# An early transpose of wqkv, kept in DRAM, and three more row buffers

## The chip, the cores and the metric

The kernel runs on one core of a Trainium2 chip. The metric is device time in microseconds (us) from launch to end of the program. The core has five engines with a queue each: TensorE (PE, matrix products; PEld is its weight load), VectorE (DVE), ScalarE (ACT), GpSimd (POOL) and SyncE (SP, which computes nothing). SP, POOL and ACT also start DMA transfers, which 16 DMA engines carry out. An instruction that waits holds everything behind it on its own queue.

## The reference

A transformer block and its gradients: sliding-window attention (32 heads of 16, a window of 8 positions two apart), then a GELU feed-forward, with 2048 positions and width 512, in bf16.

```python
qkv = (layernorm(x) @ wqkv)            # q, k, v of 32 heads
logits = q[s] . k[s - 2*w] * scale     # w = 0..7, masked where s - 2*w < 0
o = sum_w softmax(logits)[w] * v[s - 2*w]
h  = x + o @ wo
h2 = h + gelu(layernorm(h) @ w1 + b1) @ w2 + b2
# returned: h2 and, from grad_out, the gradients of x, wqkv, wo, w1, b1, w2, b2
```

The backward part is what the change touches. For each position the gradients of q, k and v are window sums: products of attention weights (or of their gradients) with rows of k, q or grad-of-o, summed over the window. Then `gx = gq @ wq^T + gk @ wk^T + gv @ wv^T`, which needs `wqkv` transposed, and the gradient of `wqkv` is `layernorm(x)^T` times these gradients.

## The kernel before

The 2048 positions are cut into four chunks of 512 (`c` = 0 to 3). A tile framework places the instructions: the program names tiles with a pool, a tag and a number of buffers, the framework adds the semaphore waits, and a scheduler orders each engine's queue. `high_priority` moves some matmuls ahead, and `gate(ins, key)` makes one instruction wait for a marked one, so that a transfer does not begin too early. Pools are stacks of memory on a left and a right side; a tile of a later pool may lie where a released one lay, and then waits for its last readers.

The order of the work:

- Forward, by chunk: layernorm, qkv, attention, output projection, feed-forward. `wqkv` stands in SBUF with its columns reordered; after the second last attention chunk it is written to `wqkv_d` in DRAM (line 580).
- Backward through the feed-forward: `b1_gg(i)` (lines 660 to 697) goes over seven pairs of hidden tiles. For each it loads `bu` and `bs` on POOL's queue (four buffers each), makes the GELU derivative on ACT and DVE (the ACT instruction of line 675 is marked `("y", i, f2)`), multiplies with a TensorE product, transposes the result on TensorE and stores it as `h1tm_d` on POOL's queue. `b1_gx(i)` is the product with `w1` transposed and the layernorm backward. Between them `gw2_gen` makes the gradient of `w2`; each of its 14 steps loads a transposed `gtm` on SP's queue (two buffers) and is 16 matmuls.
- Backward through the output projection: `b_go(c)`, with `woT`, a DMA transpose of `wo` made by `load_T` (line 725).
- Backward through the softmax: `b_ga(c)` (line 743). It loads `v4` and `go4` (named `bv` and `go` in the profile, one buffer each), makes 2 x 4 products `pag` on DVE in four buffers of tag `prA`, sums them on TensorE into `ga`, and turns them into `gl` by four DVE operations, lines 753 to 757.
- Window sums: `b_sum(c, sel)` (line 836). `sel` 2 is the value gradient (rows `go_r`), 0 the query gradient (rows `k_r`), 1 the key gradient (rows `q_r`). Each has a load of weights `ba` (two buffers; 16 small DMAs in all for `sel` 0) and four row loads `r4` (`r` in the profile, 576 KB each, `W4B` = 5 buffers of tag `w4`). Each row tile gives two DVE products of 1.2 us (`pb`, line 330) and eight matmuls (line 336).
- `b_gx(c)` (line 867) multiplies the three gradients with `wqkvT` (`psy`, line 881) and goes back through layernorm; `gwqkv_gen` and `gwo_gen` make weight gradients and, with `gw1_gen` (line 769), fill TensorE between the sums.

The loop of lines 921 to 929 does `sel` 2 for all chunks, with `b_ga(2)` after the last step of chunk 0 and `b_ga(3)` after step 1 of chunk 2; `take(wg)` places one step of `gw1_gen` per sum step. At the first step of chunk 2 it issues the load of `wqkvT` on SP: one DMA transpose of all of `wqkv_d`, 512 x 1536, gated on a copy of `gw1_gen`. After chunk 2 `load_otm` issues two loads of 1 MB on POOL. `wqkvT` lies in pool `bg`, which exists from line 828 on, when the transposed feed-forward weights are released. Pool `bp2` (line 934) lies where `bt` and `bm` lay, which hold operands of `gw1_gen` and of `b_ga`; its first loads wait for their last readers.

Of the kernel before, what the change touches and what calls it, by code (L numbers as in the profile page):

```python
# [10 lines left out]
P = 128  # L11
BF16 = mybir.dt.bfloat16
# [23 lines left out]
def kernel(  # L36
# [74 lines left out]
    def gate(ins, key):  # L111
        behind(ins, mark[key])
# [36 lines left out]
    h1tm_d = dram.tile([S, F], BF16, name="h1tm_d")  # L149
    gq_d = [[dram.tile([CH, D], BF16, name=f"gq_d{s}_{c}") for c in range(NC)] for s in range(3)]  # L150
    wqkv_d = dram.tile([D, 3 * D], BF16, name="wqkv_d")
    wo_d = dram.tile([D, D], BF16, name="wo_d")

    def tm(ap2d):
# [377 lines left out]
    def mix(gen, gen2, steps=1):  # L532
        for _ in gen:
            take(gen2, steps)
        take(gen2, 100)
# [163 lines left out]
    def b1_gx(i):  # L699
        c = b1_order[i]  # L700
        t1s = gh1.pop(c)
        for j in range(TC):
            ps = acc(f"psx{c}_{j}", "L" if i < NC - 1 else "B")
            for ft in range(FT):
                nc.tensor.matmul(ps[:], lhsT=t1s[ft // 2][:, ft % 2, j * P:(j + 1) * P], rhs=w1T[:, ft, :],  # L705
                                 start=(ft == 0), stop=(ft == FT - 1))
            t = c * TC + j
            ln_bwd(ps[:], ln2a[:, c, j, :], rstd2[:, t:t + 1], gout[c][:, j, :], gh[c][:, j, :], f"f{t}")
            yield
# [13 lines left out]
    ln2a = bm.tile([P, NC, TC, D], BF16, name="ln2a")  # L723

    def load_T(t_, d_t, key):
        gate(sync.dma_start_transpose(out=t_[:], in_=d_t[:, :]), key)

    def b_go(c):
        ghT = get(bm, [P, DC, CH], BF16, f"ghT{c}", "ghT", 1)
# [13 lines left out]
    def b_ga(c):  # L743
        v4 = feat4(bm, v_r, PAD + CJ * c - HALO, CJ + HALO, f"bv4_{c}", "k4", 1, ga_key.get(c))
        go4 = feat4(bm, go_r, CJ * c, CJ, f"go4_{c}", "q4", 1, ga_key.get(c))
        gl = get(bm, [P, Q4, TC, 2 * H], BF16, f"gl{c}", "gl", 1)
        for i in range(TC // 2):
            ga = ltile(f"ga{c}_{i}")
            dots(bm, ga, go4, v4, i, f"g{c}_{i}")
            g4 = ga[:].rearrange("p j (w h) -> p j w h", w=W)  # L750
            a4 = attn_v(c, i)
            pr = bm.tile([P, 2, W, H], F32, name=f"sp{c}_{i}", tag="e", bufs=2)
            nc.vector.tensor_tensor(out=pr[:], in0=g4, in1=a4, op=ALU.mult)
            rs = const.tile([P, 2, H], F32, name=f"rs{c}_{i}", tag="rs", bufs=2)
            nc.vector.tensor_reduce(out=rs[:], in_=pr[:].rearrange("p j w h -> p j h w"), axis=AX.X, op=ALU.add)
            nc.vector.tensor_tensor(out=pr[:], in0=g4, in1=rs[:].unsqueeze(2).to_broadcast([P, 2, W, H]), op=ALU.subtract)
            nc.vector.tensor_tensor(out=pair_v(gl, i), in0=a4, in1=pr[:], op=ALU.mult)
        put_q(pq, gl_r, c, gl[:].rearrange("p s j m -> p s (j m)"))
# [33 lines left out]

    load_ln2a(0)
    mix(b1_gx(0), none)
    for i in range(1, NC):
        load_ln2a(i)
        for n, _ in enumerate(b1_gg(i)):
            take(gw2, 1 if n in (2, 5) else 0)
            if n == 3 and i == 1:
                load_T(woT, wo_d, ("y", 1, 3))  # L800
        if i == NC - 1:
            br2.release()
            bt = pool("bt", 1)
            load_tmx(0, 2)
            load_tmx(2, 4)
            mix(b_go(0), none)
            b_ga(0)
        for n, _ in enumerate(b1_gx(i)):
            take(gw2, 1 if n == 1 else 0)
        if i > 1:  # L810
            mix(b_go(3 if i == 2 else 1), none)
# [24 lines left out]
    def b_sum(c, sel):  # L836
        sg = 0 if sel == 0 else 1
        d_a = at_r if sel == 2 else gl_r
        d_r, t_r = ((k_r, PAD - 2), (q_r, 0), (go_r, 0))[sel]
        nja = CJ + 2 * sg  # L840
        a4 = att4(bs_, d_a, CJ * c, nja, f"ba{sel}_{c}", "ba", 2, sg)
        gt = gvt[c] if sel == 2 else bp.tile([P, TC, D], BF16, name=f"gt{sel}_{c}")
        gts[sel, c] = gt
        for qd in range(Q4):
            r4 = row4(bs_, d_r, qd, t_r + CJ * c, CJ + 2, f"r4_{sel}{c}{qd}", "w4", W4B, sg)
            ps = acc(f"pss{sel}{c}_{qd}", "A")
            wsum(bs_, ps, a4, r4, sg, f"{sel}{c}_{qd}", 200)
            o_ap, i_ap = gt[:, :, qd * P:(qd + 1) * P], ps[:].rearrange("p (j m) -> p j m", j=TC)
            if sel == 2:
                mark["s", c, 2] = mark["s", c, 2, qd] = nc.scalar.copy(out=o_ap, in_=i_ap)  # L850
            else:
                mark["s", c, sel] = nc.scalar.activation(out=o_ap, in_=i_ap, func=ACT.Copy, scale=scale)  # L852
            yield
# [67 lines left out]
    for c in range(NC):  # L921
        for n, _ in enumerate(b_sum(c, 2)):
            take(wg)
            if c == 2 and n == 0:
                load_T(wqkvT, wqkv_d, ("ow1", 2, 2))
            if (c, n) in ((0, 3), (2, 1)):
                b_ga(2 + c // 2)
        if c == 2:
            load_otm()
    mix(wg, none)  # L930
    bt.release()
    bm.release()
# [66 lines left out]
```

## Time and profile before

| | |
|---|---|
| Time, median of 7 runs | 734.33 us |
| Lowest and highest | 730.05 and 736.39 us |
| The profiled execution: time / span of its instructions | 735.18 / 732.9 us |
| PE busy | 622.3 us (85%), 3551 matmuls |
| DVE busy | 554.9 us (76%) |
| ACT / POOL busy | 388.1 / 208.3 us |
| Mean granted TensorE clock | 0.959 of full speed |
| DMA | 163.57 MB, mean 223 GB/s |

Times in a profile are from the start of the span. "Busy" leaves out DMA issues, semaphores and register work. In a timeline each line gives start, duration, engine, source line, operation and "output<-inputs", with the number of instructions merged into it; a bracket gives the idle time of the engine before it and what ended it. `SPq` is SP's queue: its durations are the time the queue spent on issuing, not the transfer's. "To landing" is the time from a DMA's issue to its end. The DMA share is the mean busy share of the 16 DMA engines; it can exceed 1, since packets overlap.

The row products stand from 512 to 691 us; the feed-forward backward from about 290 to 460.

### The profile page before, as it was taken

How to read it: one execution, taken by the hardware profiler on the slowest of the kernel's cores; microseconds unless marked ns; L12 is line 12 of the kernel's file. 1: busy time of each engine (PE TensorE's matmuls, PEld its weight loads, DVE VectorE, ACT ScalarE, POOL GpSimd, SP SyncE). 2: the span in 40 equal slices, each digit the busy share in tenths (PEclk: the TensorE clock that was granted, in tenths of full speed). 3: DMA queues.
4: the chain of work that ended last, by engine and by line, in shares of the span. 5: the costliest groups of instructions: out<-in, count | busy, mean ns of one | idle time of the engine just before them, and what ended most of it. 6: DMA issues, size and time to landing. Idle time of an engine off the chain costs nothing. (4 is left out here: it accounts for less than half of the span.)

```text
span 732.9 us, 10118 instructions
## 1 busy us (share of the span) xinstructions
PE 622.3 (85%) x3551; PEld 261.7 (36%) x3618; DVE 554.9 (76%) x919; ACT 388.1 (53%) x540; POOL 208.3 (28%) x316
## 2 busy tenths in 40 slices
PE   1897658779697798999999899979993897999996
PEld 0332223233242244444444444434331232334442
DVE  6467957789967769759888884766983797999945
ACT  4653425859846489548766784521310132557553
POOL 4234333525524334443424333132002020000100
PEclk9999887999999899999999999999998899999999
DMA  8597698748986598586749969497899578996562
GB/s 226 142 272 219 199 383 280 247 176 276 341 175 222 192 225 206 165 306 143 222 125 161 182 172 243 126 205 276 309 216 340 194 236 287 345 313 205 171 140 64
DMA packets 110788, 163.57 MB, mean 223 GB/s; under 512 B 69169, under 2 KB 77458, under 8 KB 110738
## 3 DMA queue, kind: packets, MB, share of 16 engines
q1 hardware_dynamic: 81936, 79.97, 41.5%
q0 software_dynamic: 24176, 78.50, 33.6%
q10 hardware_dynamic: 4626, 4.46, 2.2%
q8 instruction: 28, 0.46, 0.2%
q14 instruction: 22, 0.18, 0.1%
HBM read 88.87 MB, written 56.71 MB: 199 GB/s over the span
## 5 line engine op out<-in xcount | busy, mean ns | idle before, releaser
L330 DVE TENSOR_TENSOR pb<-ba,r 128x2048 bf16<-128x2048 bf16 x96 | 111.5, 1217 | 15.2 <-DMA r<-go_r 9.9
L492 PE MATMUL psf<-ln2T,w 128*128 128x512 bf16 x218 | 56.3, 388 | 5.9 <-ACT u L494 5.1
L653 PE MATMUL psw<-gout,gtm 128*128 128x512 bf16 x202 | 51.5, 386 | 7.6 <-DMA gtm<-g_d 6.3
L777 PE MATMUL psw<-h1tm,ln2a 128*128 128x512 bf16 (+1 forms) x249 | 56.3, 366 | 0.7 <-issue 0.5
L521 PE MATMUL ps<-w,g 128*128 128x512 bf16 x217 | 56.0, 383 | 0.3
L705 PE MATMUL psx<-w1T,gh 128*128 128x512 bf16 x211 | 49.8, 379 | 0.3
L330 DVE TENSOR_TENSOR pbo<-a,v 128x2048 bf16<-128x2048 bf16 x32 | 38.4, 1216 | 12.1 <-DMA a<-at_r 8.0
L372 ACT CAST qkv<-psq 128x512 bf16<-128x512 f32 x48 | 27.6, 586 | 33.1 <-PE psq L370 27.1
L313 DVE TENSOR_TENSOR pag<-go,bv 128x2048 bf16<-128x2048 bf16 x24 | 28.4, 1216 | 21.1 <-PE ga L320 11.0
L336 PE MATMUL pss<-pb,sel 128*32 128x512 bf16 x384 | 30.0, 389 | 14.0 <-DVE pb L330 13.6
L683 PE MATMUL psg<-goutT,w2T 128*128 128x512 bf16 x161 | 41.2, 379 | 0.4
L494 ACT ACTIVATE u<-psf,b1c 128x512 bf16<-128x512 f32 x56 | 36.2, 681 | 7.5 <-PE psf L492 6.2
L852 ACT ACTIVATE gt<-pss 128x512 bf16<-128x512 f32 x32 | 19.1, 598 | 32.3 <-PE pss L336 30.4
L777 PEld LDWEIGHTS <-ln2a 128*128 128x128 bf16 x256 | 23.2, 100 | 36.3 <-issue 20.0
L696 POOL DMA_DIRECT2D h1tm_d<-th x27 | 20.6, 765 | 54.4 <-ACT th L694 49.1
L504 ACT ACTIVATE s<-z 128x1024 bf16<-128x1024 bf16 x28 | 29.4, 1057 | 10.2 <-DMA s_d<-s 5.2
L492 PEld LDWEIGHTS <-w 128*128 128x128 bf16 x224 | 20.8, 99 | 35.0 <-issue 16.7
L694 ACT COPY th<-pth 128x1024 bf16<-128x1024 bf16 x27 | 27.0, 1000 | 11.4 <-PE pth L692 11.3
L336 PE MATMUL pso<-pbo,sel 128*32 128x512 bf16 x128 | 17.4, 459 | 17.6 <-DVE pbo L330 15.3
L675 ACT ACTIVATE by<-bu 128x1024 bf16<-128x1024 bf16 x21 | 22.2, 1055 | 18.9 <-DVE gb1p L685 16.6
L881 PE MATMUL psy<-wqkvT,gT 128*128 128x512 bf16 x121 | 30.9, 379 | 0.6 <-DVE lua L639 0.2
L913 PE MATMUL psq<-gt,ln1a 128*128 128x512 bf16 x123 | 31.1, 380 | 0.3 <-issue 0.2
(214 smaller groups left out, 1344.5 us busy)
## 6 DMA issues: line engine op xcount, KB each, us to landing
v<-v_r SPq DMA_DIRECT2D x16, 576.0 KB, 6.4
r<-go_r SPq DMA_DIRECT2D x16, 576.0 KB, 8.3
r<-k_r SPq DMA_DIRECT2D x16, 576.0 KB, 6.5
r<-q_r SPq DMA_DIRECT2D x16, 576.0 KB, 5.5
g_d<-g POOLq DMA_DIRECT2D x28, 256.0 KB, 3.9
h1tm_d<-th POOLq DMA_DIRECT2D x27, 256.0 KB, 4.1
h1tm<-h1tm_d POOLq DMA_DIRECT2D x3, 2048.0 KB, 11.8
x_d<-u POOLq DMA_DIRECT2D x21, 256.0 KB, 5.0
```

The lines of the kernel that those rows point to most:

```text
L330: last = nc.vector.tensor_tensor(out=pr[:], in0=_ap(a_ap, [a_ap.ap[0], [2 * H, CJ], [0, Q4], [1, H]], off=wh * H + (4 * H * wh if sg else 0)),
L336: mm = nc.tensor.matmul(ps[PR * n:PR * n + PR, :], lhsT=sel4[:], rhs=prs[wh][:, TC * n:TC * n + TC, :, :].rearrange("p j d h -> p (j d h)" ...
L492: nc.tensor.matmul(ps[:], lhsT=w1[0][:, dc, ft * P:(ft + 1) * P], rhs=ln2T[:, dc, :], start=(dc == 0), stop=(dc == DC - 1))
L494: nc.scalar.activation(out=u[:, i, :], in_=ps[:], func=ACT.Identity, bias=b1c[:, ft:ft + 1], scale=1.0)
L504: nc.scalar.activation(out=s[:], in_=z[:], func=ACT.Sigmoid, scale=2.0 * GC)
L521: nc.tensor.matmul(ps[:], lhsT=gs[ft // 2][:, ft % 2, j * P:(j + 1) * P], rhs=w2[0][:, ft, :], start=(ft == 0), stop=False)
L653: nc.tensor.matmul(ps[:], lhsT=gtm[:, t, :], rhs=gout[t // TC][:, t % TC, :], start=(t == 0), stop=(t == NT - 1))
L683: nc.tensor.matmul(ps[:], lhsT=w2T[:, dc, ft * P:(ft + 1) * P], rhs=gT[:, dc, :], start=(dc == 0), stop=(dc == DC - 1))
L705: nc.tensor.matmul(ps[:], lhsT=t1s[ft // 2][:, ft % 2, j * P:(j + 1) * P], rhs=w1T[:, ft, :], start=(ft == 0), stop=(ft == FT - 1))
L777: nc.tensor.matmul(ps[:, 0:nf * P], lhsT=ln2a[:, t // TC, t % TC, dc * P:(dc + 1) * P], rhs=tmx[:, t, 0:nf * P], start=(t == 0), stop=(t = ...
L881: nc.tensor.matmul(ps[:], lhsT=gT[sel][:, g, j * P:(j + 1) * P], rhs=wqkvT[:, sel * G + g, :], start=(n == 0), stop=(n == NJ - 1))
L913: nc.tensor.matmul(ps[:], lhsT=ln1a[:, t // TC, t % TC, dc * P:(dc + 1) * P], rhs=gts[sel, t // TC][:, t % TC, :], start=(t == 0), stop=(t ...
```

## The change

Two things are changed.

The load of `wqkvT` by one DMA transpose in the loop of window sums is gone. In its place `turn_w` transposes the three thirds of `wqkv_d` one after the other on SP's queue, in step 1 of `b1_gg(1)`, into three of the four buffers of tag `prA` of pool `bm` (the buffers that the dot products of `b_ga` use later), each gated on `("y", 1, 0)`. POOL's queue stores each to a DRAM tile `wT_d`. After chunk 2 of the value sums, three plain loads on POOL's queue bring them to `wqkvT`; they are gated on a new mark, `("g", 3, 0)`, the first product of the softmax backward of chunk 3.

For query and key sums (`sel` 0 and 1), three of every eight row tiles now come from a new tag `w4x` with three buffers in pool `bp2`; the other five stay with tag `w4`, which has five buffers as before.

```diff
+    wT_d = [dram.tile([P, DC * D], BF16, name=f"wT_d{s}") for s in range(3)]
...
     def load_T(t_, d_t, key):
-        gate(sync.dma_start_transpose(out=t_[:], in_=d_t[:, :]), key)
+        gate(sync.dma_start_transpose(out=t_[:], in_=d_t if isinstance(d_t, bass.AP) else d_t[:, :]), key)
...
-            nc.vector.tensor_tensor(out=pr[:], in0=g4, in1=a4, op=ALU.mult)
+            mark["g", c, i] = nc.vector.tensor_tensor(out=pr[:], in0=g4, in1=a4, op=ALU.mult)
...
+    def turn_w():
+
+        for sel in range(3):
+            t_ = bm.tile([P, DC, D], BF16, name=f"wT{sel}", tag="prA", bufs=PRA)
+            load_T(t_, wqkv_d[:, sel * D:(sel + 1) * D], ("y", 1, 0))
+            pq.dma_start(out=wT_d[sel][:, :], in_=t_[:].rearrange("p c d -> p (c d)"))
+
     for i in range(1, NC):
         load_ln2a(i)
         for n, _ in enumerate(b1_gg(i)):
             take(gw2, 1 if n in (2, 5) else 0)
+            if n == 1 and i == 1:
+                turn_w()
             if n == 3 and i == 1:
                 load_T(woT, wo_d, ("y", 1, 3))
...
         for qd in range(Q4):
-            r4 = row4(bs_, d_r, qd, t_r + CJ * c, CJ + 2, f"r4_{sel}{c}{qd}", "w4", W4B, sg)
+            p_, tag, n_ = (bs_, "w4", W4B) if sel == 2 or next(turn) % 8 < 5 else (bp, "w4x", 3)
+            r4 = row4(p_, d_r, qd, t_r + CJ * c, CJ + 2, f"r4_{sel}{c}{qd}", tag, n_, sg)
...
         for n, _ in enumerate(b_sum(c, 2)):
             take(wg)
-            if c == 2 and n == 0:
-                load_T(wqkvT, wqkv_d, ("ow1", 2, 2))
             if (c, n) in ((0, 3), (2, 1)):
                 b_ga(2 + c // 2)
         if c == 2:
             load_otm()
+            for sel in range(3):
+                gate(pq.dma_start(out=wqkvT[:, sel * DC:(sel + 1) * DC, :], in_=wT_d[sel][:, :].rearrange("p (c d) -> p c d", c=DC)),
+                     ("g", 3, 0))
```

## The prediction

> **What bounds the kernel now.** I read the page first (busy shares, the 40 slices), then busy time by stretch, then the timelines of SyncE, VectorE and TensorE around the moved transfer, then the waits of the GpSimd queue where the new work is put. No engine is full over the whole span (TensorE 85%, VectorE 76%), so the stage decides. The first view is busy time by stretch; columns are start:end, length, busy of PE, weight loads, DVE, ACT, POOL, granted clock, DMA share, GB/s.
>
> ```profile
> 512.00:527.50 15.50, 15.29 (x107) 6.04 (x107) 14.78 (x14) 5.06 (x9) 2.22 (x4) 1.00 0.84 297
> 550.00:593.00 43.00, 28.41 (x138) 9.37 (x139) 25.64 (x27) 4.69 (x8) 4.53 (x6) 0.84 0.73 237
> 593.00:632.00 39.00, 33.12 (x250) 12.37 (x254) 33.69 (x31) 15.93 (x25) 4.33 (x8) 1.00 0.92 312
> 632.00:690.00 58.00, 57.40 (x408) 22.93 (x415) 57.94 (x72) 31.78 (x55) 3.02 (x4) 1.00 0.81 264
> ```
>
> Between 512 and 690 us the window sums run (value gradients first, `b_sum(c,2)` with `b_ga(2)` and `b_ga(3)`, then key rows, then query rows). Before 527 and after 632 both PE and DVE are full; in 550 to 593 both stand idle for a third of the time. The timeline of SP's queue says what happens there:
>
> ```profile
> 524.37 0.57 SPq L282 DMA_DIRECT2D r<-go_r  x1
> 527.47 22.01 SPq L726 DMA_TRANSPOSE wqkvT<-wqkv_d  x1
> 549.57 1.83 SPq L282 DMA_DIRECT2D r<-go_r  x3
> 552.16 0.55 SPq L282 DMA_DIRECT2D bv<-v_r  x1
> 555.28 0.51 SPq L282 DMA_DIRECT2D go<-go_r  x1
> ```
>
> The 1.5 MB transpose holds SP for 22.01 us; the next three row loads leave within 1.83 us of its end, so their buffers had long been free. Then the timelines of DVE and, below it, PE; in brackets the idle time before the instruction and what ended it:
>
> ```profile
> 556.49 1.23 DVE L330 TENSOR_TENSOR pb<-ba,r 128x2048 bf16<-128x2048 bf16 x1 [9.22 <-DMA r<-go_r]
> 569.34 4.63 DVE L313 TENSOR_TENSOR pag<-go,bv 128x2048 bf16<-128x2048 bf16 x4 [7.23 <-DMA go<-go_r]
> 578.43 1.23 DVE L313 TENSOR_TENSOR pag<-go,bv 128x2048 bf16<-128x2048 bf16 x1 [3.33 <-PE ga L320]
> 616.75 9.17 DVE L330 TENSOR_TENSOR pb<-ba,r 128x2048 bf16<-128x2048 bf16 x8 [3.24 <-DMA r<-k_r]
> ```
>
> ```profile
> 559.83 1.04 PE L336 MATMUL pss<-pb,sel 128*32 128x512 bf16 x8 [8.43 <-DVE pb L330]
> 570.62 0.59 PE L320 MATMUL ga<-pag,sel 128*32 128x512 bf16 x1 [5.83 <-DVE pag L313]
> 573.49 2.31 PE L777 MATMUL psw<-h1tm,ln2a 128*128 128x512 bf16 x5
> ```
>
> The first two waits are for loads behind the transpose; the third is PE coming back at half clock (five matmuls in 2.31 us there, 1.25 us elsewhere).
>
> **What the Trainium skill says.** (1) "DMA: Bandwidth & Descriptors", section "Anatomy of one DMA — SWDGE (gpsimd) path": a DMA engine waits for no semaphore, the issuing sequencer does, before it dispatches. So a DMA that waits holds all that is behind it on its queue; the trace agrees (row loads stuck 22 us). (2) The same page, "Issuing engines are not separate DMA queues": all queues share 16 engines, so a load moved to POOL saves SP's issue time, not bandwidth. Agrees: the DMA share is 1.12 in 527.5 to 550. (3) "Advanced Engine Details and Errata", section "X-Bar Transpose (TRN2)": transposes at 350-400 GB/s. The trace does not agree: 1.57 MB in 22 us of issue is 71 GB/s. (4) "TensorE: Matmul & The Clock Gate", "What's actually happening": half clock after about 3.4 us idle. Agrees: clock 0.50 in 558 to 562.
>
> **The change part by part.** I sum against the profiled execution (735.18 us, span 732.9), which is 0.85 us above the median of 734.33.
>
> *1. The transpose leaves SP at 527.* From 546.58 to 593.41 (last value work, first key row) DVE has 46.83 us, of which waits are 9.22 + 7.23 + 3.33 + 0.32 = 20.1 and work 26.7. What is late next: `go_3`/`bv_3`. Their one buffer is free when the last dot product of `b_ga(2)` ends, at 543.9. In the new order the first dot product of `b_ga(3)` stands only four row products and three small operations after it: 4 x 1.15 + 0.60 + 0.95 + 0.60 = 6.7 us, so at 550.6. The pair for `b_ga(2)` was issued at 521.76 and used at 529.78, 8.0 us; the median landing of `go` in 520 to 600 is 7.4. Issued at about 544.5 it is there at 552 to 553: a wait of 1 to 4 us, I take 2.5. I leave 1 us for the 2 MB `h1tm` and the two 1 MB `botm` loads crossing row loads. Gain 20.1 - 3.5 = 16.6 us; bounds 11 (the wait for `go_3` stays at its 7.2 and 2 us more are lost) and 19. PE can follow: in 550 to 632 it loses 8.43 + 5.83 + 0.22, then 1.54 + 3.37 + 0.28, and about 4.5 to the half clock (21 matmuls took 5.0 us from 559.8 and 16 took 6.9 us from 570.6, where they take 3.6 and 3.8 at full clock), 24 in all, more than the sum wants.
>
> *2. Three plain loads on POOL instead* (0.5 MB each, gate: first softmax-gradient product of `b_ga(3)`, near 580 before, about 560 now). Behind them on POOL stand only the `gl_r` stores of chunk 3 and the four `ln1a` loads; the gate opens before DVE has made that `gl`, so none is held. Estimate of DMA time: 1.57 MB at the 381 to 399 GB/s that the fullest stretches show, 4 us. DMA is 0.73 busy in 550 to 593, so it fits. The first reader of `wqkvT` is at 625.6, about 606 then: slack 40 us. Cost 0; within the 1 us above.
>
> *3. Three more row buffers.* In 593 to 632 DVE waits 1.76 + 3.24 + 0.31 = 5.3 us for key rows. Five buffers hold 5 x 2.3 = 11.5 us of products against a landing of 6.5 (key rows, page) to 10.1 us (value rows there). With eight it is 18 us. But the four little loads of `ba` (2.4 us of issue) still stand in the order and wait for the buffer of two chunks ago, and the first row into a new buffer waits for the last `gw1` matmul (589.5 before, about 572 now), some 4 us ahead of the first key product. Also rows plus `ln1a` want about 13.6 MB (16 rows of 0.59, four `ba` of 0.26, 2.1 of `ln1a`, eight stores of 0.13) in 32 x 1.15 = 37 us, 0.37 MB/us, near what DMA gives. Bounds 0 and 5.3; I take 3. From 632 on nothing is to be had: PE 57.40 and DVE 57.94 of 58.
>
> *4. The early transposes.* Gate `("y",1,0)` falls at 298.5, so SP's order decides: they follow `ln2a` at 312.01, stand ahead of `k_first<-v_r` (wanted at 467) and of `woT` (issued 337.58, wanted at 411). Three at 2.1 (`woT`) to 8.4 us (longest `gtm`) of issue each end at 319 to 337; landing 7.7 (`woT`) to 18.9. Behind them POOL gets three stores that wait for them. The first fence is busy time by stretch again (columns as above), the second POOL's timeline:
>
> ```profile
> 331.00:334.00 3.00, 2.95 (x19) 1.38 (x19) 2.62 (x9) 2.26 (x5) 0.00 (x0) 1.00 0.00 0
> ```
>
> ```profile
> 335.87 0.77 POOL L696 DMA_DIRECT2D h1tm_d<-th  x1 [12.10 <-ACT th L694]
> ```
>
> DMA is empty from 328 to 337 and POOL idle from 323.8 to 335.9: that is the cover. The next POOL load with a date is the `bu` of step 6: issued 337.91, landing 5.2, read by ACT at 348.60, slack 5.5 us. So until about 341 the hold is free. `gtm` for step 2 was issued at 342.4 and is wanted by PE at 361.49, slack 19 less a landing of 7.7 to 18.9; the 1.57 MB of stores (4 us of DMA) come beside it where the DMA share is above 1. Below: nothing. Above: third landing at 337 - 8.4 + 18.9 = 348, hold 12, less slack 5.5, so 7 us. I take 1, since PE is full there and pays all that is late.
>
> *5. No cost:* the dot products' buffers are used early but not again before 467; VectorE work is the same, two value products change places; SP's order moves one row ahead of `bv_3` and one key row ahead of `ba`, within part 3's bounds.
>
> Sum: -16.6 - 3 + 1 = -18.6; 735.2 - 18.6 = 716.6 by the profiled execution, 715.7 by the median. I say 716.
>
> **The rivals.** A, the feed takes over: DMA is 0.86 busy over 512 to 690 already, and a shorter stage needs the same bytes sooner; rows come late, the wait for `go_3` stays long. For: 0.92 in the key stage. Against: DMA share 0.07, 0.19, 0.00 in 578 to 590. Part 1 gives 8 to 10, part 3 nothing: 735 - 9 + 1 = 727. B, early jam: part 4 at its upper end, with one half-clock start: 716 + 9 = 725. C, slower: the three early transposes crawl as the old one did in its second half, and the POOL queue stands behind the third store. Each us after 341 that the third lands is paid whole by the full TensorE stage; as the gain is 18.6, this turns the sign if it lands after about 361, 49 us after its start, a rate under half of the 71 GB/s seen. With a landing at 370 it gives 716 + 29 - 1 = 744. Against: nine empty us of DMA. D, nothing moves: the hole is taken over whole by the 2 MB `h1tm` load of 532.3, which landed after 21.5 us: 734. Against: that load shared the engines with the transpose.
>
> **How the numbers follow.** Forecast 0.62 (709 to 721), A 0.17, B 0.07, C 0.09, D 0.05. The upper bounds of parts 1, 3 and nothing in part 4 give 735 - 19 - 5.3 = 711, less 1 to 2 if the half clock goes too: low end 709. The high end takes in A and B, 729. A measurement of this kernel can tell about 0.5% (3.7 us) from no change. Faster by more: the forecast, A, B and a little of D, 0.86; same 0.04; slower 0.10.
>
> **What would show it.** Part 1: no transpose on SP near 527, row loads issued there without a gap, DVE's waits in 545 to 580 below 5 us together, granted clock 1.00. Part 2: `wqkvT` landed long before the first `psy`. Part 3: waits for key rows under 3 us. Part 4: DMA no longer empty at 328 to 337, POOL's wait for the transposes ending by 341, PE at 411 (first `psgo`) within 1 us. It is wrong if the row products still wait 8 us or more in one place after 545, or if the first `psgo` comes more than 5 us later.

## The result, and the profile after

The changed kernel takes 728.06 us (median of 27 runs, single ones between 720.04 and 744.05) against 734.59 us for the kernel before (median of 64); the ratio is 0.9897, with a 95% interval of 0.9874 to 0.9920. So it is about 1% faster. A ratio compares only executions within 1.5% of the fastest of their kernel, medians take in all, and the profiles of e4, e9 and e14 below come from executions beyond that bound. The forecast had the direction, and the time lies inside its range of 709 to 729, but it said 716: of 18.6 us expected, some 7 came.

The profiled execution of the changed kernel took 728.27 us, with a span of 726.4 us. Two landmarks that both kernels have cut the span into three stretches: the load of `ln2a` on SP (issued before anything that the change touches) and the first `psgo` matmul (the first work after the stage that holds the early transposes). First before, then after:

```profile
312.01 0.35 SPq L791 DMA_DIRECT2D ln2a<-ln_d  x1
410.99 1.03 PE L735 MATMUL psgo<-woT,ghT_first 128*128 128x512 bf16 x4
```

```profile
307.30 0.35 SPq L792 DMA_DIRECT2D ln2a<-ln_d  x1
421.42 1.91 PE L736 MATMUL psgo<-woT,ghT_first 128*128 128x512 bf16 x4
```

| us | start to load of `ln2a` | `ln2a` to first `psgo` | first `psgo` to end | span |
|---|---|---|---|---|
| before | 312.0 | 99.0 | 321.9 | 732.9 |
| after | 307.3 | 114.1 | 305.0 | 726.4 |
| difference | -4.7 | +15.1 | -16.9 | -6.5 |

The first stretch runs the same program in both kernels; in the fifteen profiled executions with this forward it lies between 304.4 and 312.0, so its difference is chance. The other two are the change: the end gained what was promised, the middle gave nearly all of it back.

The late part first. Busy time by stretch of the changed kernel (start:end, length, busy PE, weight loads, DVE, ACT, POOL, granted clock, DMA share, GB/s), the last three of the windows shown of before:

```profile
550.00:593.00 43.00, 42.42 (x248) 15.32 (x256) 40.84 (x42) 9.16 (x16) 8.38 (x13) 1.00 0.91 299
593.00:632.00 39.00, 32.82 (x246) 11.80 (x243) 32.64 (x30) 14.98 (x24) 2.15 (x4) 1.00 0.92 328
632.00:690.00 58.00, 57.40 (x406) 23.80 (x413) 56.04 (x76) 34.67 (x59) 3.02 (x4) 1.00 0.70 230
```

From 550 to 593 us PE went from 28.41 to 42.42 busy of 43 and DVE from 25.64 to 40.84, at full clock. SP's timeline there has no transpose any more, only loads:

```profile
534.96 7.38 SPq L283 DMA_DIRECT2D r<-go_r  x4
...
556.86 21.74 SPq L283 DMA_DIRECT2D r<-go_r  x3
```

The waits of DVE over 1 us from 530 us on (the bracket is the idle time before the instruction):

```profile
540.37 4.63 DVE L314 TENSOR_TENSOR pag<-go,bv 128x2048 bf16<-128x2048 bf16 x4 [1.20 <-DMA go<-go_r]
606.55 9.17 DVE L331 TENSOR_TENSOR pb<-ba,r 128x2048 bf16<-128x2048 bf16 x8 [4.91 <-issue]
617.17 23.93 DVE L331 TENSOR_TENSOR pb<-ba,r 128x2048 bf16<-128x2048 bf16 x21 [1.45 <-DMA r<-k_r]
```

The 9.22, 7.23 and 3.33 us of before are gone. The last two lines are the key stage, and there nothing was gained: 6.4 us against 5.3 (for 4.91 of it, marked "issue", the profile shows nothing that was waited for).

Now the middle. SP's timeline of the changed kernel:

```profile
307.75 22.00 SPq L727 DMA_TRANSPOSE wT<-wqkv_d  x3
329.91 0.57 SPq L283 DMA_DIRECT2D k_first<-v_r  x1
332.96 7.42 SPq L727 DMA_TRANSPOSE woT<-wo_d  x1
340.48 79.35 SPq L651 DMA_TRANSPOSE gtm<-g_d  x6
```

The three transposes hold SP as long as the single one did at 527. By 332 us the last has landed and POOL issues its third store (332.27), well inside the 341 us up to which I had called the hold free. What is late comes after that. Busy time by stretch, first of the kernel before, then of the changed one:

```profile
330.00:360.00 30.00, 29.56 (x175) 13.59 (x178) 26.71 (x62) 22.86 (x27) 12.90 (x18) 1.00 0.72 193
360.00:400.00 40.00, 39.30 (x222) 19.02 (x226) 33.46 (x76) 28.71 (x38) 15.72 (x22) 1.00 0.73 146
```

```profile
330.00:360.00 30.00, 24.92 (x139) 11.32 (x140) 22.22 (x50) 17.62 (x20) 12.60 (x18) 0.93 1.11 209
360.00:400.00 40.00, 34.09 (x174) 15.67 (x177) 26.09 (x59) 23.89 (x32) 12.21 (x17) 0.93 1.17 139
```

Look at the last two columns together. From 360 to 400 us the DMA engines are "busy" 1.17 instead of 0.73 and move less, 139 GB/s against 146: each byte keeps an engine busy longer. I call this the crawl, and read it as packets that wait, though the records do not show for what. PE lost 9.9 us of busy time in these two windows. Its waits, from its timeline, name two things that are late; the third line, of ACT, says what held up the first:

```profile
357.77 0.26 PE L693 MATMUL pth<-ident,gh 128*128 128x128 bf16 x1 [4.65 <-ACT th L695]
369.17 5.31 PE L654 MATMUL psw<-gout,gtm 128*128 128x512 bf16 x16 [5.05 <-DMA gtm<-g_d]
356.71 1.01 ACT L695 COPY th<-pth 128x1024 bf16<-128x1024 bf16 x1 [4.51 <-DMA h1tm_d<-th]
```

`th` has three buffers, freed by the stores to `h1tm_d` (median landing 7.0 us, 4.1 before), and `gtm` comes by DMA transpose. After the second wait 16 matmuls take 5.31 us, where such a group takes 3.62 in e1 below; the granted clock from 369 to 375 us was 0.72. The transposes of `gtm` from 335 to 420 us, before and after (the first line has min/median/max issue time in ns, the second the us from issue to landing):

```profile
L650 SPq DMA_TRANSPOSE gtm<-g_d x6: 2068/2848/8367, 342.4 to 405.6; - x6
...
DMA to landing us min/median/max: 7.7/16.9/18.9
```

```profile
L651 SPq DMA_TRANSPOSE gtm<-g_d x6: 3071/8081/18102, 340.5 to 415.4; - x6
...
DMA to landing us min/median/max: 12.8/19.0/26.5
```

The packet records of the trace say it most plainly. A transpose of 0.5 MB is 2,048 packets of 256 B. In the kernel before, `woT` and the next three `gtm` ran from first to last packet in 4.8, 2.7, 3.9 and 3.3 us, and only then came three of 9.2, 13.8 and 10.4 us. In the changed kernel `wT` took 3.4, 12.5 and 2.0 us, and then `woT` and six `gtm` took 12.5, 16.4, 13.1, 12.1, 9.4, 12.7 and 9.9 us, one behind the other with pauses of at most 2.6 us between the `gtm`. So the crawl is not new: in the kernel before it begins at 384 us, 72 us after the load of `ln2a`, and costs PE little (the longest wait for a `gtm` there is 2.35 us); in the changed kernel `woT` is in it already at 337 us, 30 us after that load.

### The profile page after: what moved, and what is told of

The parts are those of the page before. It is cut to its first block, busy times and chain, and to the rows that moved or that the text cites. A ratio compares the mean times of both kernels' runs of the same rounds, so it can differ in the third digit from the quotient of the medians.

```text
span 726.4 us, 10116 instructions
## 1 busy us (share of the span) xinstructions
PE 622.5 (86%) x3551; PEld 261.9 (36%) x3618; DVE 555.0 (76%) x919; ACT 387.6 (53%) x540; POOL 211.9 (29%) x322
## 5 line engine op out<-in xcount | busy, mean ns | idle before, releaser
L654 PE MATMUL psw<-gout,gtm 128*128 128x512 bf16 x202 | 53.5, 398 | 12.1 <-DMA gtm<-g_d 10.8
L778 PE MATMUL psw<-h1tm,ln2a 128*128 128x512 bf16 (+1 forms) x249 | 53.4, 353 | 0.5 <-issue 0.3
L706 PE MATMUL psx<-w1T,gh 128*128 128x512 bf16 x211 | 51.9, 391 | 0.3
L695 ACT COPY th<-pth 128x1024 bf16<-128x1024 bf16 x27 | 27.0, 1001 | 16.4 <-PE pth L693 9.2
L654 PEld LDWEIGHTS <-gtm 128*128 128x128 bf16 x208 | 19.9, 101 | 39.0 <-DMA gtm<-g_d 12.6
L778 PEld LDWEIGHTS <-ln2a 128*128 128x128 bf16 x256 | 22.6, 98 | 27.8 <-issue 10.3
L706 PEld LDWEIGHTS <-gh 128*128 128x128 bf16 x216 | 21.4, 101 | 29.9 <-issue 7.6
## 6 DMA issues: line engine op xcount, KB each, us to landing
h1tm<-h1tm_d POOLq DMA_DIRECT2D x3, 2048.0 KB, 12.1
```

Source lines behind the costliest of these rows:

```text
L654: nc.tensor.matmul(ps[:], lhsT=gtm[:, t, :], rhs=gout[t // TC][:, t % TC, :], start=(t == 0), stop=(t == NT - 1))
L778: nc.tensor.matmul(ps[:, 0:nf * P], lhsT=ln2a[:, t // TC, t % TC, dc * P:(dc + 1) * P], rhs=tmx[:, t, 0:nf * P], start=(t == 0), stop=(t = ...
```

## The experiments

The question: what made the middle stretch 15 us longer? Theory T: each transposed byte takes its toll on the traffic of this stage. Theory P: their place is the cost, since SP's other transposes come later and out of step. (The expectations also name H1 to H3, Q, S, V and F, each explained in its text.) The rivals: the stores (their 1.57 MB, or POOL's wait for them, which was the forecast's own mechanism), and the load of `v` that was pushed behind. All stretches are of the one profiled execution of each run; ratios are to the kernel before, measured beside it.

| run | median us (runs) | ratio, 95% interval | `ln2a` to first `psgo` | `psgo` to end |
|---|---|---|---|---|
| e1 no wqkv transpose | 708.83 (4) | 0.9694 (0.9641-0.9747) | 96.4 | 303.1 |
| e16 the same again | 713.27 (6) | 0.9779 (0.9729-0.9829) | 96.5 | 305.5 |
| e2 transposes, no stores | 728.36 (20) | 0.9838 (0.9800-0.9877) | 107.0 | 304.9 |
| e3 plain loads and stores | 716.16 (4) | 0.9774 (0.9726-0.9822) | 96.3 | 305.7 |
| e4 old row buffers | 729.72 (14) | 0.9920 (0.9881-0.9960) | 114.9 | 306.2 |
| e5 transposes one by one | 718.69 (4) | none given | 104.7 | 304.7 |
| e6 in the forward, DMA | 720.87 (4) | 0.9834 (0.9750-0.9919) | 95.7 | 305.5 |
| e7 in the forward, PE | 727.24 (15) | 0.9878 (0.9842-0.9914) | 101.2 | 299.5 |
| e8 late, three pieces | 726.94 (12) | 0.9908 (0.9874-0.9941) | 96.6 | 318.9 |
| e9 `v` loaded first | 725.56 (19) | 0.9831 (0.9789-0.9872) | 111.7 | 305.1 |
| e10 only `woT` later | 715.34 (4) | 0.9772 (0.9733-0.9810) | 101.0 | 304.1 |
| e11 quiet stretches | 714.62 (6) | 0.9746 (0.9695-0.9796) | 101.8 | 306.0 |
| e13 first quiet stretch | 718.18 (6) | 0.9761 (0.9689-0.9833) | 97.1 | 308.5 |
| e14 stores later | 731.49 (12) | 0.9836 (0.9767-0.9905) | 117.1 | 303.4 |
| e15 e1 without part 3 | 714.21 (6) | 0.9760 (0.9704-0.9816) | 98.8 | 304.6 |

e1 and e16 are one kernel, measured on two chips: its ratio moved by 0.9%, nearly the width of an interval, so differences below 1% between groups are not read from ratios. Its middle stretch moved by only 0.1 us, but that is too good a measure of the scatter. The kernel before, e8 and e15 have no early transposes either, and show 99.0, 96.6 and 98.8; e6 and e7, behind a changed forward, show 95.7 and 101.2. So a middle stretch without the early part takes 96 to 101 us, and what lies within that is not read as a cost.

### What the early part costs, and which half of it (e1, e2, e3)

e1, no transpose of `wqkv` at all:

```diff
-            if n == 1 and i == 1:
-                turn_w()
...
-                gate(pq.dma_start(out=wqkvT[:, sel * DC:(sel + 1) * DC, :], in_=wT_d[sel][:, :].rearrange("p (c d) -> p c d", c=DC)),
+                gate(pq.dma_start(out=wqkvT[:, sel * DC:(sel + 1) * DC, :], in_=wqkv_d[:, sel * D:(sel + 1) * D].rearrange("(c p) d -> p c d", p=P)),
```

> The changed kernel without the early transposes and their three stores; wqkvT is loaded plain and untransposed from wqkv_d by the same three POOL loads at the same place, so the transpose is left out of the computation. It prices the early part and shows what parts 1 to 3 are worth alone. Theory (the early part gave back some 14 us): first psgo at about 407, value stage as in the changed kernel, time 712 to 716 (0.970 to 0.975 of before). Rival (the late stage gains less than its waits suggest, and the early part is nearly free): 724 to 728, with the first psgo at 420.

Measured: 708.83 us, middle stretch 96.4 us. So the early part costs 17.7 us of middle stretch (114.1 - 96.4) by these profiles, 13 to 18 against all the executions without it, and 9 to 15 us by the ratios (0.9897 less 0.9779 or 0.9694, of 734). By the medians, each divided by that of the kernel before beside it, it is 13 to 18 us. In e1 and e16 alike, parts 1 to 3 alone end below the 716 of the forecast. e2 keeps the transposes and drops their stores (`wqkvT` is loaded untransposed, as in e1):

```diff
-            pq.dma_start(out=wT_d[sel][:, :], in_=t_[:].rearrange("p c d -> p (c d)"))
```

> As the last, but with the three early transposes on SP kept and only their stores to DRAM left out (what they fetch is not used; wqkvT is loaded untransposed). Theory H1 (the transposes themselves make the DMA crawl from 330 to 400): first psgo near 420, time 726 to 729, the same as the changed kernel. Rival H2 (the 1.57 MB of stores meet woT, gtm and h1tm_d): first psgo near 408, time 712 to 717. In between, say 720, would say that bytes in flight as such count (H3).

e3 puts plain loads of the same bytes in their place and keeps the stores, from which `wqkvT` comes untransposed:

```diff
-            load_T(t_, wqkv_d[:, sel * D:(sel + 1) * D], ("y", 1, 0))
+            gate(sync.dma_start(out=t_[:], in_=wqkv_d[:, sel * D:(sel + 1) * D].rearrange("(c p) d -> p c d", p=P)), ("y", 1, 0))
```

> The changed kernel with the three early transposes replaced by plain loads of the same bytes on the same queue; the stores to DRAM stay and wqkvT comes from them untransposed, so the transpose is left out. H1 (transposes): 712 to 717 with first psgo near 408. H2 (stores): 726 to 729 with first psgo near 420. H3 (bytes as such): near 720.

e2 came to 728.36 us (median) and 107.0 us of middle stretch, e3 to 716.16 us and 96.3 us. The bytes are free: loads and stores of 1.57 MB each cost nothing there. The transposes do cost, without any store: 10.6 us of middle stretch over e1 in the profiled execution of e2. That execution, 722.85 us, is among the faster of its 20; the median of e2 is that of the changed kernel (728.06), as theory H1 said. So the 7.1 us between the two stretches (114.1 - 107.0) may be the stores, beside transposes, or the scatter of a crawl; these runs don't tell. The same two windows in e1 and e2:

```profile
330.00:360.00 30.00, 29.72 (x169) 13.69 (x166) 26.82 (x62) 22.43 (x28) 15.63 (x22) 1.00 0.82 227
360.00:400.00 40.00, 39.37 (x238) 19.30 (x236) 33.01 (x76) 27.51 (x36) 15.08 (x21) 1.00 0.85 145
```

```profile
330.00:360.00 30.00, 26.06 (x134) 11.27 (x133) 22.39 (x53) 18.51 (x21) 10.19 (x15) 0.90 1.13 177
360.00:400.00 40.00, 37.15 (x201) 17.68 (x200) 29.56 (x67) 25.64 (x34) 15.02 (x21) 0.95 1.05 162
```

Without stores the DMA share is still above 1, PE still loses 5.9 us in the two windows against e1, and the granted clock falls to 0.90 and 0.95: the crawl comes with the transposes, without the stores.

### The stores' share: POOL's wait, or bytes? (e14)

```diff
+            if n == 5 and i == 1:
+                for sel in range(3):
+                    gate(pq.dma_start(out=wT_d[sel][:, :], in_=wTs[sel][:].rearrange("p c d -> p (c d)")), ("y", 1, 5))
```

(the transposes stay in `turn_w`; their tiles are kept in `wTs`.)

> The changed kernel with its three stores to DRAM gated to a later step (the square of step 5 of the second chunk), so that POOL does not stand waiting for the transposes; the transposes stay where they are. Nothing is left out. It divides what the stores add to the transposes (first psgo 114 us after the load of ln2a against 107 without stores). If it is POOL's wait of 12 us behind them, as the forecast had it: back to 106 to 108 us, ratio 0.981 to 0.986. If it is their 1.57 MB in a stage in which the DMA already crawls: 112 to 116 us, ratio 0.988 to 0.992.

Measured: 731.49 us (median of 12), ratio 0.9836 (0.9767 to 0.9905). The interval covers both answers. In its profiled execution (730.79 us, middle stretch 117.1) POOL waits for no early transpose any more, but one wait is traded for another:

```profile
373.48 0.76 POOL L697 DMA_DIRECT2D h1tm_d<-th  x1 [10.70 <-DMA wT_d<-wT]
```

By the profile POOL stands 10.70 us until one of the stores has landed, ACT waits 13.7 us for a `bs`, and PE loses 11.0 us behind it. Open: whether the stores beside the transposes cost anything through POOL's wait or through their bytes.

### The load of v that was pushed behind (e9)

```diff
+        v4s[0] = feat4(bm, v_r, PAD - HALO, CJ + HALO, "bv4_0", "k4", 1)
```

(as the first thing in `turn_w`, and taken from there in `b_ga(0)`.)

> The changed kernel with one load moved on SP: the 960 KB of v for the first gradient of the attention weights, which in the changed kernel comes right behind the three transposes (329.91 us, in the kernel before it was issued before 313), is issued ahead of them. Nothing is left out. Theory V (this load, pushed behind the transposes, meets woT and starts the crawl): ratio 0.978 to 0.982 (717 to 720). Theories P and T: within 0.3% of the changed kernel, 0.987 to 0.992.

Measured: 725.56 us (median of 19), 0.9831 (0.9789 to 0.9872). It ends just below the changed kernel's interval (0.9874). If this load matters, it is by about 0.7%, less than e1 and e16 differ by; that is not settled. That it is not what starts the crawl, its profiled execution (729.48 us) shows: with `v` ahead `woT` took only 3.4 us, but the next four `gtm` took 12.8, 18.1, 16.8 and 8.0 us from 344 us on, and the middle stretch is 111.7 us.

### Is it only that the other transposes come later? (e10)

That is theory Q, the plain half of P. e10 is e1, without a transpose of `wqkv`, but `woT` begins some 7 us later (32.8 us after the load of `ln2a` in place of 25.5), and one `gtm` that stood behind it now goes ahead:

```diff
-                load_T(woT, wo_d, ("y", 1, 3))
+                load_T(woT, wo_d, ("th", 1, 2))
```

(with `mark["th", i, f2]` set at the eviction of `th`.)

> The first run's kernel (no transpose of wqkv at all; wqkvT is loaded untransposed) with one wait more: the transpose of wo begins after the eviction th of step 2 instead of the square of step 3, about 6 us later, and so stands behind a gtm transpose, not ahead of it. Theory Q (what costs is only that woT and the gtm transposes come some microseconds later and then fall upon the traffic of the backward steps): first psgo 103 to 108 us after the load of ln2a, ratio 0.978 to 0.985. Theory T (the 1.57 MB of transposes itself, not the place of woT): as in the first run, 96 to 98 us and a ratio of 0.967 to 0.973.

Measured: middle stretch 101.0 us, between the 96 to 98 of T and the 103 to 108 of Q. That is 4.6 us longer than in e1, but only 2.0 to 2.2 longer than in the kernel before and e15, so the length is not told from the scatter. The ratio (0.9772) doesn't tell this apart from e1 and e16 either. The transposes of `gtm`, first in e1, then in e10:

```profile
L651 SPq DMA_TRANSPOSE gtm<-g_d x6: 1928/2556/5812, 335.6 to 398.7; - x6
...
DMA to landing us min/median/max: 7.7/11.1/16.0
```

```profile
L651 SPq DMA_TRANSPOSE gtm<-g_d x6: 2297/4479/8380, 338.2 to 402.2; - x6
...
DMA to landing us min/median/max: 7.6/16.3/20.4
```

With not one byte more, the `gtm` transposes take longer to land. (PE waits 3.1 us for one; but in the kernel before and e15 it waits 2.35 and 2.0 us, too.) What lies beyond the scatter is in the packets: after `woT` the `gtm` took 14.4, 9.6, 10.3, 14.2 and 10.6 us. In e1 the same five took 3.9, 3.4, 8.4, 11.0 and 7.9, and in the kernel before, e3, e8, e15 and e16 the first two of them took 3.2 to 5.1 us as well. So in this one execution another time and order of `woT` was enough to start the crawl two transposes sooner. What that costs, and why a transpose crawls at one time and not at another, was not found.

### Other places (e5, e6, e7, e8)

e5 spreads the three over the stage, one after step 0 and step 4 of the second chunk and one after step 1 of the third:

```diff
-            if n == 1 and i == 1:
-                turn_w()
+            if (i, n) in ((1, 1), (1, 5), (2, 2)):
+                turn_w({(1, 1): 0, (1, 5): 1, (2, 2): 2}[i, n], ("y", i, n - 1))
```

> The changed kernel with its three early transposes, each with its store, at three places of the same stage instead of one: after step 0 and step 4 of the second chunk and after step 1 of the third. Nothing is left out. Theory P (what costs is that 22 us of transposes stand in one piece ahead of woT and the gtm transposes, which then queue without a gap): one piece of 5 to 8 us fits between two gtm transposes, ratio to before 0.975 to 0.980 (715 to 719). Theory T (each transposed byte takes its toll wherever it meets the traffic of this stage, since a transpose that meets other packets takes 9 to 16 us instead of 2 to 5): the same ratio as the changed kernel, 0.988 to 0.992, or worse.

Measured: 718.69 us (four runs; the kernel before beside it 735.69, so 0.977), middle stretch 104.7. Half way: P's ratio, but a stretch 8.3 us over e1's. Here POOL's wait is real, since the second store stands in the order ahead of its transpose's end: POOL's timeline has 14.11 us of idle time before it.

e6 does the transposes in the forward, through the same tag of the forward's pool, between `f_o(3)` and the release of that pool:

```diff
     f_o(3)
+    turn_w(0)
     f_h(3)
+    turn_w(1)
+    turn_w(2)
     fr.release()
```

(gated on `("o", 3, 3)`.)

> The changed kernel with its three transposes and stores moved out of the backward stage altogether: they run in the forward after the last attention chunk, through the homes of the dot products there, near 239 to 255 us on SP, ahead of the transpose of w1. Nothing is left out. Both P and T: first psgo returns to its place (some 103 us after the load of ln2a, against 114 in the changed kernel), ratio 0.970 to 0.978 (711 to 717), if the forward hides them. Rival F (the forward pays as much: w1T is pushed back by 8 us or more and the first psx waits for it): 0.985 to 0.992.

Measured: 720.87 us; the middle stretch is 95.7 us, the shortest of all, and the transposes in it take 2 to 6 us each. But the load of `ln2a` comes at 322.3 us, at least 10 later than in any run with the old forward: rival F, though the ratio (0.9834) stays just under F's range. PE's timeline shows a wait in the forward that the changed kernel hasn't, 8.22 us for `ln` at 261.06.

e7 lets TensorE do them there, behind `f_attn(3)`:

```diff
+                    nc.tensor.transpose(pt[:, (i * DC + dc) * P:(i * DC + dc + 1) * P], wqkv[:, dc, j0:j0 + P], ident[:])
+            nc.scalar.copy(out=t_[:, 2 * c2:2 * c2 + 2, :], in_=pt[:].rearrange("p (i t) -> p i t", i=2))
```

> The changed kernel with the wqkv transposes done by TensorE in the forward after the last attention chunk (48 transposes of 128x128 and six ACT evictions of 128x1024) in place of the DMA transposes; the three stores and the late loads stay. Nothing is left out. No DMA transpose of wqkv is left, so theories P and T both expect the gtm transposes to run as in the kernel before, and what is paid is at most the 48 transposes and the stores: ratio 0.972 to 0.980 (713 to 719). Above 0.985 would say that PE or ACT pays in full in the forward, or that the stores are the cost.

Measured: 727.24 us, 0.9878: a miss. `ln2a` comes at 320.7 us, as late as in e6: the forward pays some 9 to 16 us for 48 transposes and six evictions. The longest wait in it is for ACT, 7.72 us for `u` before 241.76 in PE's timeline.

The other half of the expectation failed too, and this is the more telling miss: with no DMA transpose of `wqkv` anywhere, `woT` and the `gtm` transposes took 7.5, 15.1, 6.6, 9.0, 9.7 and 11.4 us from 348 us on. The crawl came by itself, in a stage that an upset forward had shifted, though the middle stretch, 101.2 us, is only at the end of the range without the early part. Together with e10 this is two executions in which the crawl starts with `woT` or right behind it and nothing was added to this stage.

e8 goes back to the late place, in three pieces instead of one:

```diff
+            if (c, n) in ((1, 1), (2, 0), (2, 3)):
+                sel = {(1, 1): 0, (2, 0): 1, (2, 3): 2}[c, n]
+                load_T(wqkvT[:, sel * DC:(sel + 1) * DC, :], wqkv_d[:, sel * D:(sel + 1) * D], ("s", c, 2))
```

> The changed kernel without the early transposes, the stores and the three late loads: wqkv is transposed on SP straight from wqkv_d into wqkvT as in the kernel before, but in three pieces of 512 columns at three places of the value stage (chunk 1 step 1, chunk 2 steps 0 and 3). Nothing is left out. Theory S (SP has room for a hold of 2 to 5 us between two rows, with five row buffers ahead; only the piece of 22 us starved DVE): first psgo 96 to 99 us after the load of ln2a, psgo to the end 304 to 309 against 305 in the changed kernel and 322 before, ratio 0.970 to 0.978. Rival (under the traffic of the value stage, 343 GB/s, each piece takes 10 to 15 us and the rows come late again): 0.983 to 0.992.

Measured: 726.94 us, 0.9908. The middle is clean (96.6), the end 318.9 us, near the old 321.9: the rival's range, but not its reason, for it gave each piece 10 to 15 us, and from first to last packet they took 3.9, 7.4 and 3.0. They hold SP for only 3.20, 6.60 and 2.29 us, but DVE's timeline has two of the old waits again, and a longer one in the key stage, whose cause the profile doesn't show:

```profile
554.65 1.22 DVE L314 TENSOR_TENSOR pag<-go,bv 128x2048 bf16<-128x2048 bf16 x1 [5.25 <-DMA go<-go_r]
564.00 1.22 DVE L314 TENSOR_TENSOR pag<-go,bv 128x2048 bf16<-128x2048 bf16 x1 [2.98 <-PE ga L321]
605.47 6.90 DVE L331 TENSOR_TENSOR pb<-ba,r 128x2048 bf16<-128x2048 bf16 x6 [8.07 <-issue]
```

### The quiet stretch (e11, e13)

In the `dh` products (`b1_gx`) POOL issues nothing for about 10 us. e11 puts two transposes into the first such stretch and one into the second, and gates the stores to a later step:

```diff
+            if (i, n) in ((1, 0), (1, 2), (2, 0)):
+                turn_w({(1, 0): 0, (1, 2): 1, (2, 0): 2}[i, n], ("y", i, 6))
...
+            if n == 2:
+                for sel in sorted(wTs):
+                    keep_w(sel, ("y", i, 1))
```

> The changed kernel with its three transposes put where POOL issues nothing for ten microseconds, in the two stretches of dh products behind the second and the third chunk's feed-forward gradients (two of them in the first, one in the second), each store a few steps later, gated so that POOL never waits for a transpose. Nothing is left out. Theories P and T both: the transposes take 2 to 4 us each, first psgo 96 to 100 us after the load of ln2a, ratio 0.969 to 0.977 (711 to 717). If instead each transposed byte costs wherever it is, 107 us and 0.983 to 0.990.

Measured: 714.62 us, 0.9746. The first two took 4.0 and 2.2 us; the third stood behind crawling `gtm` transposes, and POOL's timeline shows what that cost:

```profile
418.51 0.56 POOL L805 DMA_DIRECT2D wT_d<-wT  x1 [13.94 <-DMA wT<-wqkv_d]
```

The stretch is 101.8 us, above the 96 to 100 that was expected. e13 puts all three into the first quiet stretch (the edit is against e11):

```diff
-            if (i, n) in ((1, 0), (1, 2), (2, 0)):
-                turn_w({(1, 0): 0, (1, 2): 1, (2, 0): 2}[i, n], ("y", i, 6))
+            if i == 1 and n < 3:
+                turn_w(n, ("y", 1, 6))
```

> The kernel of the last run (transposes in the quiet stretches, stores gated) with the third transpose moved from the second quiet stretch, where it took 13 us behind a crawling gtm transpose and held POOL for 13.9 us, into the first: all three between 347 and 360 us. Nothing is left out. Theory P (they cost nothing as long as they meet little traffic and the gtm transposes behind them stay in step): first psgo 96 to 99 us after the load of ln2a, ratio 0.968 to 0.974 (711 to 715). Theory T or Q (three in one piece push the gtm transposes out of step wherever it is): 102 to 108 us, 0.976 to 0.984.

Measured: 718.18 us; middle stretch 97.1 us, as P said and within the range without the early part. The ratio, 0.9761, falls into the range of T and Q, but its interval (0.9689 to 0.9833) covers both. SP's hold in e13, and its two windows:

```profile
346.59 13.14 SPq L727 DMA_TRANSPOSE wT<-wqkv_d  x3
```

```profile
330.00:360.00 30.00, 29.71 (x173) 13.53 (x172) 26.44 (x61) 24.03 (x28) 14.17 (x20) 1.00 0.95 217
360.00:400.00 40.00, 38.98 (x225) 18.64 (x223) 33.44 (x75) 26.39 (x33) 16.68 (x25) 1.00 1.17 211
```

The same 1.57 MB, transposed in the same stage and stored through the same tiles, and PE stays full at full clock; `gtm` landed after 13.1 us in the median instead of 19.0. It is not free of the crawl: two `gtm` from 393 us on took 10.3 and 17.5 us, about when transposes crawl in the kernel before, too. A DMA share of 1.17 alone is thus no sign of a loss: at 139 GB/s it stood beside one, at 211 it did not. Theory T in its plain form falls, as far as one execution goes: the toll depends on the place. e11 and e13 both beat the kernel before and, by their intervals, the changed one; which of the two is better these runs don't tell.

### The row buffers alone (e4, e15, e16)

```diff
-            p_, tag, n_ = (bs_, "w4", W4B) if sel == 2 or next(turn) % 8 < 5 else (bp, "w4x", 3)
+            p_, tag, n_ = bs_, "w4", W4B
```

In e4 from the changed kernel, in e15 from e1, beside e16 (e1 again):

> The changed kernel with part 3 undone: query and key rows use the five old row buffers alone. Theory of the forecast (the row buffers are worth 3 us): 731 against 728 of the changed kernel (ratio to before 0.995). Rival (the key stage waits for DMA and ln1a whatever the buffers, as its waits of 6.4 us in the changed kernel against 5.3 before suggest): within 1 us of the changed kernel, ratio 0.989 to 0.991.

> The first run's kernel (no transpose of wqkv; wqkvT is loaded untransposed), which scatters least, with part 3 undone: query and key rows use the five old row buffers alone. If the three row buffers are worth the 3 us that the forecast gave them, 0.4% above its companion of the same call; if the key stage waits for other things, within 0.2% of it.

> The first run's kernel once more, beside the last one and on the same chip, for the price of part 3 alone: 0.967 to 0.972 of before, as in the first run.

e4: 729.72 us, 0.9920, and its interval covers both answers. (Up to the first `psgo` e4 is the changed kernel, and its 114.9 us are a second execution of that.) The pair e15 and e16: 714.21 us without the buffers, 713.27 us with them; the end of the span takes 304.6 and 305.5 us. Part 3 is not told from nothing. DVE's timeline says why; first e15, then e16:

```profile
589.84 4.63 DVE L331 TENSOR_TENSOR pb<-ba,r 128x2048 bf16<-128x2048 bf16 x4 [2.12 <-DMA r<-k_r]
597.84 6.90 DVE L331 TENSOR_TENSOR pb<-ba,r 128x2048 bf16<-128x2048 bf16 x6 [3.36 <-PE pss L337]
605.04 30.75 DVE L331 TENSOR_TENSOR pb<-ba,r 128x2048 bf16<-128x2048 bf16 x27 [0.30 <-DMA r<-k_r]
```

```profile
591.39 42.10 DVE L331 TENSOR_TENSOR pb<-ba,r 128x2048 bf16<-128x2048 bf16 x37 [6.04 <-DMA r<-k_r]
```

With eight buffers 37 products run without a wait, as the sum of part 3 wanted. But the first key row comes late, and the one wait of 6.04 us in front is as long as the three waits without them, 5.8 us together. (In e1, the same kernel as e16, the waits are 4.02, 0.49 and 0.60 us.)

## Why the forecast was right in direction and wrong in size

*Part 1 (-16.6) was right.* First `psgo` to the end went from 321.9 to 305.0, minus 16.9, and since part 3 gives nothing it is all part 1. All four signs came: no transpose on SP near 527, DVE's waits from 530 us on below 1.3 us each in the value stage, clock 1.00 from 550 on, and the wait for `go_3`, priced at 2.5 us, below 1. Rival A expected the feed (DMA bringing the rows) to take over here; its time, 727, came true, its reason didn't.

*Part 2 (0) shows no sign of being wrong.* The three loads were issued at 571.7 us and landed after 6.3 us in the median, and the first `psy` came at 617.6. No run leaves them out in the changed kernel, so they have no measured price of their own.

*Part 3 (-3) was too high.* The waits of the key stage are 6.4 us where I wanted under 3. The term assumed that all of the 5.3 us were for want of buffers; in the pair the buffers only gather them at the front, where the first row is late.

*Part 4 (+1, bounds 0 to 7) is the step that failed*, and with it the sum. It cost 15.1 us by the stretch against before, 17.7 against e1, 9 to 15 by the ratios and 13 to 18 by the medians: beyond its upper bound by each. The working asked when the three stores release POOL, found 5.5 us of slack behind that and called it covered until 341. That event came at 332.8, in time, and priced nothing. The mechanism was another: the transposes hold SP until 329.75, `woT` and `gtm` come behind them, and from 337 us on they run at 9 to 16 us a piece, where in the kernel before the first four take 3 to 5 and only the last three 9 to 14, with stores of `h1tm_d` and loads of `bs` (median landing 10.4 us, 5.8 in e1) slowed beside them. That the transposes start this, and bytes and stores without transposes don't, e1, e2 and e3 show; how they do it stays open. I had seen slow landings ("beside it where the DMA share is above 1"), but priced only the moved transfers' own, not what they do to the transposes already there. Test and size: first `psgo` was to come within 1 us; it came 10.4 us later in the span though its stage had begun 4.7 us sooner. With the measured terms the sum is -16.9 + 15.1 = -1.8 by the profiled executions, to which chance in the forward adds -4.7; the medians, in which such chance should cancel, differ by 6.5. So one of the stretches of the two profiled executions is some 5 us off the usual, and which one is not known: the end of the span and the middle of the kernel before were profiled once. A long middle in the changed kernel is no accident of one execution, since e4, e9 and e14, with transposes at the same place, have 114.9, 111.7 and 117.1 us.

That the time lies inside the range of 709 to 729 is luck as far as the forecast goes: its own end was 721, and rivals A and B stretched the range. Rival C named the crawl and hung it on POOL's third store; the crawl came, without a late store. Rival B put part 4 at its upper end, 725, near in time, but by the same hold of POOL. Two readings set beside the Trainium skill were loose: the row loads at 527 stood behind 22 us of issue, not behind a DMA that waited, and a DMA share of 1.12 shows busy engines, not that queues share them; that POOL's stores slow down beside SP's transposes (7.0 us to landing against 4.1) speaks for it more directly. The Trainium skill gives transposes 350 to 400 GB/s ("Advanced Engine Details and Errata", section "X-Bar Transpose (TRN2)"). In the forward of the changed kernel, with no other packets under way, 0.5 MB of the transpose of `w2` took 1.8 us from first to last packet, some 290 GB/s, not far off. In the crawl the same amount took up to 16.4 us, 32 GB/s. I had averaged this into one rate of 71 GB/s, which describes neither.

## What to carry to other kernels

Moving a DMA transpose off the critical stretch is only half a price; the other half is what it does to the transposes that are already where it lands, so look for a stretch in which the other queues issue nothing, as in e13. Compare the DMA share with GB/s: a share above 1 with few bytes marked the crawl here (1.17 at 139 GB/s). It does not say what the crawl costs: the kernel before has 1.09 at 143 GB/s from 383 to 394 us, with PE 10.75 busy of 11. And where landmarks cut the span so that only one part of a change lies in each piece, the pieces tell the parts apart in a single profile, when the totals scatter by more than the parts are worth; but the same stretch without the early part took 96 to 101 us in different executions, so a single profile is no proof for a few us.

## What was not expected of the hardware

- 0.5 MB of transpose took 1.8 us alone, 3 to 5 us beside 79 to 105 GB/s of other traffic in one phase (the kernel before, 339 to 371 us), and 9 to 16 us beside 57 to 175 GB/s in another (the changed kernel, from 337 us on). In the kernel before, at 384 us, it took 9.2 us beside only 62 GB/s.
- The crawl passes from one transpose to the next: seven in a row in the changed kernel, from 337 to 429 us, and as many in e7 from 348 us on; in e6 none of seven takes more than 6.1 us.
- Plain loads and stores of the same bytes at the same place cost nothing (96.3 us against 96.4).
- With three transposes of 2 to 7 us of SP hold each, spread over the value stage, the end (318.9 us) is nearly as long as with one of 22 us (321.9).
